# A residual block with Winograd convolutions: columns split by parity, two of six row positions also transformed along columns, PSUM emptied by ScalarE in bf16

## The chip, the cores and the metric

The kernel runs on one core of a Trainium2 chip. The metric is the time of one execution of the whole program on the device, in microseconds; lower is better. Of the kernel before the change there are three timed runs and one execution recorded by the hardware profiler. The engines are named as in the profile: PE is the matrix engine TensorE, PEld its weight loads, DVE is VectorE, ACT is ScalarE, POOL is GpSimd, SP is the engine that issues most transfers.

## What is computed

One residual block of a diffusion network: group norm, SiLU and a 3x3 convolution, an embedding added per channel, group norm, SiLU and a second 3x3 convolution, and the input added at the end. x is [2, 512, 64, 64] in bf16, with 4 groups of 128 channels.

```
def conv3(z, w):
    zp = jnp.pad(z, ((0, 0), (0, 0), (1, 1), (1, 1)))
    taps = [jnp.einsum("bchw,oc->bohw", zp[:, :, i:i+H, j:j+W], w[:, :, i, j]) for i in range(3) for j in range(3)]
    ...
h = conv3(_silu(gn(x, g1, be1)), w1)
h = h + (_silu(t_emb) @ w_emb).reshape(B, C, 1, 1)
h = conv3(_silu(gn(h, g2, be2)), w2)
return x + h
```

## The kernel before

Both convolutions are Winograd transforms F(4,3) along rows: of each six rows of input six combined rows ("positions" 0 to 5) are made, multiplied by six combined weight rows, and the six products are combined into four output rows. Along columns nothing is transformed: the three column taps `kx` are three matmuls with shifted inputs. The channels are cut into four input tiles (`ct`) and four output tiles (`ot`) of 128, each image into two chunks of 32 rows, which are eight row groups. The loops run over the two layers (0 and 1 in the code; "first" and "second" in words), in each over four chunks (two images of two chunks), and over four output tiles. One output tile of one chunk is 6 positions x 4 `ct` x 3 `kx` = 72 matmuls of 128 x 128 by 512 columns (`mm`, L628), accumulated in six PSUM accumulators of one bank each (`ps_acc`, 6 buffers, one per position). There are 32 such tiles.

Beside the matmuls run these parts:

- `prep_U` (L288 to L352) makes the combined weights of one (`ot`, `ct`): a load, nine transposes on PE (L299, L302), two ACT copies out of PSUM (L303, L305), six DVE operations (L328 to L336). The U tiles of a whole layer stay resident.
- `produce_V` (L386 to L473) makes the six positions of one chunk's input: a load of 33 rows (of x, or of the intermediate `h_scr` in HBM), one silu on ACT with the group norm's scale and bias (L415) into one of two buffers `a_tmp`, and 14 DVE operations per `ct` (L454 to L472; in the first chunk L434 to L451, where ACT does the scalings). V tiles are double-buffered.
- `evac` (L632 to L702) empties the accumulators and makes four output rows: ACT copies positions 1 and 3 out as f32 (L635, L649), DVE does the rest in f32 with ten operations (14 in the second layer, where x is added: L674, L675, L678, L681). In the first layer DVE also sums (`accum_out`) and one ACT pass squares (L697); the result goes to `h_scr`. In the second it goes to the output (L702).
- Statistics of the first image (`stats0`) are products on PE (L199 gram, L206 column sums), for the first `ct` a sum on ACT (L212), with a short chain DVE, POOL, DVE that ends in `sc_all` and `nb_all` (L163 to L181). Those of the second image (`gn1_stats_bg`) are 16 ACT passes of 2048 elements (L212, L216).

The order of the work: `_Background` holds generators with a deadline and runs a step of them between two accumulators (`tick`), at a rate that the deadlines set. Then a list scheduler orders each engine's instructions, so that some of them stand ahead of their place in the program. The queue of each engine is worked off in that order. For the first output tile of all, the matmuls go `ct` by `ct` through all six accumulators, so that PE can begin with the first input tile; in all others, position by position.

## Time and profile before

| what | value |
|---|---|
| time, median of three runs | 566.75 us (566.36 to 567.83) |
| span of the profiled execution | 564.7 us |
| first and last matmul of L628 | starts 26.3 us, ends about 558.7 us |
| end of the first output tile | 47.5 us |
| chunks of the first layer begin at | 26.3, 101.1, 169.0, 232.0 us |
| the second layer begins at | 297.4 us |

The span is what the profiler saw of one execution; the timed runs include some 2 us around it. In a row of the profile's groups, "out<-in 128x512" is a tile's name and its shape, "x16" a count, and after the bar stand the busy time and the mean duration. Rows of one engine may overlap: where instructions follow each other without a gap, the distance of their starts is less than the duration that is shown for one.

### The profile page before, as it was taken

What the parts mean: (1) busy time and instruction counts of PE and PEld (TensorE: products, weight loads), DVE (VectorE), ACT (ScalarE), POOL (GpSimd) and SP (SyncE); (2) the same over time, 40 slices, a digit from 0 to 9 for tenths busy, and PEclk for the clock granted to TensorE, in tenths of its full rate; (3) what the DMA queues carried; (4) which work ended last, traced back from release to release, by engine and by line L of the source; (5) the groups of instructions that cost most, each with busy time, mean ns of one, the idle gap of its engine ahead of it and who ended that gap; (6) DMA issues with size and microseconds to landing.
All of it is one profiled execution on the core that took longest, in us unless ns stands there. A gap on an engine that the chain in (4) does not pass through costs nothing.

```text
span 564.7 us, 7699 instructions
## 1 busy us (share of the span) xinstructions
PE 540.7 (96%) x2814; PEld 259.3 (46%) x2814; DVE 479.8 (85%) x1226; ACT 218.3 (39%) x252; POOL 23.3 (4%) x74
## 2 busy tenths in 40 slices
PE   4879999899999999999999989999999999999995
PEld 4535544344444444444445545444444444444442
DVE  2889999989988884898879999999999998555665
ACT  5699999463435332343235314322230300000000
POOL 1110000011001100000000011000000000000000
PEclk9999999999999999999999999999999999999999
DMA  8506654333523120132133512323433122222210
GB/s 336 207 22 216 192 176 139 137 114 124 161 76 108 56 105 37 45 127 96 42 101 102 160 37 76 112 80 123 153 102 101 47 75 74 75 74 76 74 39 37
DMA packets 18754, 59.83 MB, mean 106 GB/s; under 512 B 2075, under 2 KB 3227, under 8 KB 18331
## 3 DMA queue, kind: packets, MB, share of 16 engines
q1 hardware_dynamic: 18656, 59.32, 31.5%
q8 instruction: 22, 0.36, 0.3%
q14 instruction: 17, 0.14, 0.1%
q10 hardware_dynamic: 59, 0.01, 0.0%
HBM read 42.54 MB, written 16.78 MB: 105 GB/s over the span
## 4 chain that ended last, share of the span: by engine, by line
PE 72%; DVE 21%; issue 2%; DMA 2%; ACT 1%; POOL 1%; SPq 0%; DVEq 0%; ACTq 0%
PE acc L628 70%; DVE U L336 2%; DVE U L334 2%; DVE U L329 1%; DMA xbuf<-in_x_dram 1%; DVE U L330 1%; POOL rstd L178 1%; DVE cc L333 1%; PE pa L299 1%; ACT V_146 L212 1%; DMA wn<-in_w_dram 1%; DVE vq L455 1%; DVE yst L662 1%; DVE tt L666 1%; DVE ss L667 0%
## 5 line engine op out<-in xcount | busy, mean ns | idle before, releaser
L628 PE MATMUL acc<-V,U 128*128 128x512 bf16 x2016 | 444.9, 381 | 2.6 <-DVE V L457 1.6
L628 PEld LDWEIGHTS <-U 128*128 128x128 bf16 x2304 | 224.0, 98 | 273.4 <-issue 7.0
L628 PE MATMUL acc<-V_146,U 128*128 128x512 bf16 x288 | 66.4, 381 | 3.2 <-DVE V_146 L448 3.1
L697 ACT ACTIVATE junk<-yst 128x2048 bf16<-128x2048 bf16 x16 | 30.5, 1909 | 58.5 <-DVE yst L693 53.2
L303 ACT COPY U<-pa 128x768 bf16<-128x768 bf16 x32 | 25.7, 803 | 41.1 <-PE pa L299 41.1
L415 ACT ACTIVATE a_tmp_105<-src,nb_all,sc_all 128x2112 bf16<-128x2112 bf16 x14 | 30.1, 2152 | 22.2 <-DVE V L470 18.9
L415 ACT ACTIVATE a_tmp_106<-src,nb_all,sc_all 128x2112 bf16<-128x2112 bf16 x14 | 30.1, 2151 | 21.5 <-DVE vq L455 10.4
L299 PEld LDWEIGHTS <-wn 128*128 128x128 bf16 x192 | 16.5, 142 | 8.0 <-issue 2.9
L299 PE MATMUL pa<-ident,wn 128*128 128x128 bf16 x192 | 16.9, 225 | 2.6 <-DVE tot L165 2.3
L334 DVE SCALAR_TENSOR_TENSOR U<-g1t,cc 128x384 bf16<-128x384 bf16 x32 | 17.5, 546 | 0.0
L333 DVE SCALAR_TENSOR_TENSOR cc<-U 128x384 f32<-128x384 bf16 x32 | 17.5, 546 | 0.0
L336 DVE SCALAR_TENSOR_TENSOR U<-g1t,cc 128x384 bf16<-128x384 bf16 x32 | 17.5, 546 | 0.0
L305 ACT COPY g1t<-pb 128x384 bf16<-128x384 bf16 x32 | 15.8, 495 | 0.4 <-DVE U L336 0.4
L216 ACT ACTIVATE xt<-xt 128x2048 bf16<-128x2048 bf16 x8 | 15.4, 1928 | 0.1
L212 ACT ACTIVATE xt<-xt 128x2048 bf16<-128x2048 bf16 x8 | 15.4, 1928 | 0.0
L199 PE MATMUL gr<-xbuf 128*128 128x128 bf16 x96 | 7.5, 243 | 6.5 <-DMA xbuf<-in_x_dram 6.5
L693 DVE SCALAR_TENSOR_TENSOR yst<-acc,ss 128x512 bf16<-128x512 f32 x16 | 10.9, 682 | 2.5 <-PE acc L628 2.5
L457 DVE TENSOR_TENSOR V<-vq 128x528 bf16<-128x528 bf16 x28 | 11.8, 422 | 0.0
L472 DVE TENSOR_TENSOR V<-V,vq 128x528 bf16<-128x528 bf16 x28 | 11.8, 421 | 0.0
L464 DVE TENSOR_TENSOR V<-vs,vq 128x528 bf16<-128x528 bf16 x28 | 11.8, 421 | 0.0
L466 DVE TENSOR_TENSOR V<-vs,vq 128x528 bf16<-128x528 bf16 x28 | 11.8, 421 | 0.0
L469 DVE TENSOR_TENSOR V<-V,vq 128x528 bf16<-128x528 bf16 x28 | 11.8, 421 | 0.0
(660 smaller groups left out, 594.6 us busy)
## 6 DMA issues: line engine op xcount, KB each, us to landing
wn<-in_w_dram SPq DMA_DIRECT2D x32, 288.0 KB, 3.1
src<-h_scr SPq DMA_DIRECT2D x16, 528.0 KB, 3.9
h_scr<-yst SPq DMA_DIRECT2D x16, 512.0 KB, 2.6
xr<-in_x_dram SPq DMA_DIRECT2D x16, 512.0 KB, 4.1
out_dram<-yst SPq DMA_DIRECT2D x16, 512.0 KB, 3.6
src<-in_x_dram SPq DMA_DIRECT2D x12, 528.0 KB, 4.5
xt<-in_x_dram SPq DMA_DIRECT2D x8, 512.0 KB, 3.7
xbuf<-in_x_dram SPq DMA_DIRECT2D x3, 1024.0 KB, 6.2
```

The costliest lines, as they stand in the source:

```text
L212: nc.scalar.activation(out=o, in_=pc, func=ACT.Identity, accum_out=part[:, k:k + 1])
L216: nc.scalar.activation(out=pc, in_=pc, func=ACT.Square, scale=float(HW) ** -0.5, accum_out=part[:, k:k + 1])
L299: nc.tensor.transpose(pa[:, kx, j, :], wn_v[:, kx, 2 * j, :], ident[:])
L303: nc.scalar.copy(out=U[:, :, 0:NPOS:NPOS - 1, :], in_=pa[:])
L305: nc.scalar.copy(out=g1t[:], in_=pb[:])
L333: nc.vector.scalar_tensor_tensor(out=cc[:], in0=g0, scalar=0.25, in1=g2, op0=ALU.mult, op1=ALU.add)
L334: nc.vector.scalar_tensor_tensor(out=U[:, :, 3, :], in0=g1t[:], scalar=0.5, in1=cc[:], op0=ALU.mult, op1=ALU.add)
L336: nc.vector.scalar_tensor_tensor(out=U[:, :, 4, :], in0=g1t[:], scalar=-0.5, in1=cc[:], op0=ALU.mult, op1=ALU.add)
L415: nc.scalar.activation(out=at[:, a_ - r0:b_ - r0, 1:W + 1], in_=ap, func=ACT.Silu, bias=nb_all[:, layer, b, ct:ct + 1], scale=sc_all[:, la ...
L457: nc.vector.tensor_tensor(out=Vc[:, 1], in0=p_, in1=q, op=ALU.add)
L628: nc.tensor.matmul(accs[pos][:], lhsT=U[ct][:, kx, pos, :], rhs=V[:, ct, pos, :, kx:kx + W], start=first, stop=last)
L697: nc.scalar.activation(out=junk[:], in_=yf, func=ACT.Square, scale=float(HW) ** -0.5, accum_out=ssq[:, ch:ch + 1])
```

## The change

Columns are split by parity: a row of 64 is kept as 32 even and 32 odd ones. Positions 1 and 2 are then also transformed along columns by F(2,3): four combined planes (`vw`, 32 columns each) replace three shifted products of 64 columns. Their weights (`UW`) get the matching four combinations. Positions 3, 4, 0 and 5 keep their three taps; of the taps, `kx` 0 and 2 read both parities in one matmul of 512 columns, and `kx` 1 is two matmuls of 256, each writing every second run of 32 in the accumulator.

One output tile of one chunk is now four groups. Groups 0 and 1 (`mm_w`, L587) are 16 matmuls of 256 columns each; groups 2 and 3 (`mm_d`, L603 and L609) are 16 of 512 and 16 of 256 each. Each group fills an accumulator of two banks, of which there are three. ACT copies a whole accumulator (1024 columns) to bf16 (L623, L630, L636, L644); the rest of the output transform is bf16 on DVE (L627 to L646). The sums of the first layer are two ACT passes of 2048 (L656, L657); in the second layer four ACT copies of 512 (L662) put the columns back in order, one DVE addition adds x (L665), and one transfer stores (L666).

`produce_V` works on pairs of input tiles (`cp`). In the first layer each `ct` has four silus of 512 and one of 64 for the halo row (L349, the line of a helper), in the second one of 2048 and one of 64; both `ct` of a pair lie in the one buffer `at`. Then 15 DVE operations of 1024 or 2048 elements work on the pair (L397 to L438). The V tiles (`vw`, `v34`, `v05`) have three buffers, of which a chunk uses two. `prep_U` also goes by pairs: 18 transposes, three ACT copies of 768 (L290), 11 DVE operations (L294 to L307). The buffers for weight loads and temporaries are halved in number, x of the first image lies in U buffers, and the statistics of the second image (L230, L231) load into the buffers of `produce_V`. `h_scr` is kept in the new layout, and each load of it is followed by one of the halo row (L388, L391). In the first layer all four column sums of the first image are products on PE, emptied by ACT (L495).

The diff, cut to its core:

```diff
-    upool = ctx.enter_context(tc.tile_pool(name="U", bufs=4 * CT))
-    stage = ctx.enter_context(tc.tile_pool(name="stage", bufs=4))
-    wtmp = ctx.enter_context(tc.tile_pool(name="wtmp", bufs=2))
-    vpool = ctx.enter_context(tc.tile_pool(name="V", bufs=2))
+    upool = ctx.enter_context(tc.tile_pool(name="U", bufs=CT))
+    stage = ctx.enter_context(tc.tile_pool(name="stage", bufs=2))
+    wtmp = ctx.enter_context(tc.tile_pool(name="wtmp", bufs=1))
+    vpool = ctx.enter_context(tc.tile_pool(name="V", bufs=3))
+    apool = ctx.enter_context(tc.tile_pool(name="A", bufs=1))
...
-    ps_acc = ctx.enter_context(tc.tile_pool(name="ps_acc", bufs=6, space=PSUM))
+    ps_acc = ctx.enter_context(tc.tile_pool(name="ps_acc", bufs=3, space=PSUM))
...
-            xt = stg.tile([P, hp], BF16, tag="xr")
+            xt = srcp.tile([P, CR + 2, W], BF16, tag="src")
...
+    def produce_V(layer, b, ch, resident=None):
...
+        for cp in range(CP):
+            at = apool.tile([P, 2, AT], BF16, tag="at")
...
+                        for q in range(2):
+                            silu_rows(
+                                _ap(at, i * AT + f * PL + q * HF, [(2 * PL, 2), (W, TR), (1, HF)]),
+                                _ap(sbase, m_off + 2 * f * W + q, [(W, 2), (TH * W, TR), (2, HF)]),
+                                layer, b, ct)
...
+            tq = otmp.tile([P, 2, 2, NT], BF16, tag="tq")
+            VV.tensor_scalar(out=tq[:], in0=_ap(at, 0, [(2 * PL, 2), (AT, 2), (1, NT)]),
+                             scalar1=4.0, scalar2=None, op0=ALU.mult)
+            VV.tensor_tensor(out=tq[:], in0=tq[:], in1=_ap(at, PL, [(2 * PL, 2), (AT, 2), (1, NT)]), op=ALU.subtract)
+            q_, p_ = (_ap(tq, k * 2 * NT, [(W, 2 * TR), (HF, 2), (1, HF)]) for k in range(2))
+            VV.tensor_tensor(out=rows64(layer, zrow[:, 0], 2 * TR), in0=p_, in1=q_, op=ALU.add)
+            VV.tensor_tensor(out=rows64(layer, zrow[:, 1], 2 * TR), in0=p_, in1=q_, op=ALU.subtract)
...
+            e0, o0, om, e1 = E_OFF[layer], O_OFF[layer], O_BEG[layer], E_OFF[layer] + 1
+            VV.tensor_tensor(out=vwm(1), in0=zr(e0), in1=zr(o0), op=ALU.add)
+            VV.tensor_tensor(out=vwm(2), in0=zr(o0), in1=zr(e0), op=ALU.subtract)
+            VV.tensor_tensor(out=vwm(0), in0=zr(om), in1=zr(o0), op=ALU.subtract)
+            VV.tensor_tensor(out=vwm(3), in0=zr(e1), in1=zr(e0), op=ALU.subtract)
...
+            VV.tensor_tensor(out=elo[:], in0=_ap(at, PL, [(PL, 2), (AT, 2), (1, NT)]),
+                             in1=_ap(at, 0, [(2 * PL + NT, 2), (AT, 2), (1, NT)]), op=ALU.subtract)
+            VV.tensor_tensor(out=ehi[:], in0=_ap(at, W, [(3 * PL - W, 2), (AT, 2), (1, NT)]),
+                             in1=_ap(at, PL, [(PL, 2), (AT, 2), (1, NT)]), op=ALU.subtract)
+            VV.tensor_scalar(out=e12[:], in0=elo[:, 0], scalar1=2.0, scalar2=None, op0=ALU.mult)
+            s2 = _ap(e12, 0, [(W, 2 * TR), (HF, 2), (1, HF)])
+            r_ = _ap(ehi, 2 * NT, [(W, 2 * TR), (HF, 2), (1, HF)])
+            VV.tensor_tensor(out=rows64(layer, v34[:, 0], 2 * TR), in0=r_, in1=s2, op=ALU.add)
+            VV.tensor_tensor(out=rows64(layer, v34[:, 1], 2 * TR), in0=r_, in1=s2, op=ALU.subtract)
+            yield
+            VV.tensor_scalar(out=elo[:], in0=elo[:], scalar1=4.0, scalar2=None, op0=ALU.mult)
+            VV.tensor_tensor(out=rows64(layer, v05, 4 * TR),
...
-    SLOTS = NPOS
-    MARGIN = 3
+    SLOTS = 4
+    MARGIN = 2
...
-                def mm(pos, ct, kx, first, last):
-                    nc.tensor.matmul(
-                        accs[pos][:], lhsT=U[ct][:, kx, pos, :], rhs=V[:, ct, pos, :, kx:kx + W],
-                        start=first, stop=last)
+                def mm_w(acc, pair, ct, first, last):
+                    vw = V[ct // 2][0]
+                    c = ct % 2
+                    for k, m in enumerate(pair):
+                        for s in range(2):
+                            lo = UM[m] * 2 * P + s * P
+                            nc.tensor.matmul(
+                                acc[:, k, s * HT:(s + 1) * HT], lhsT=U[:, ct, lo:lo + P],
+                                rhs=vw[:, m, s, c * TR:(c + 1) * TR, :],
+                                start=first and s == 0, stop=last and s == 1)
+
+                def mm_d(acc, which, ct, first, last):
+                    vd = V[ct // 2][1 + which]
+                    c = ct % 2
+                    for k in range(2):
+                        base = vd[:, k if which == 0 else 1 - k]
+                        row = c * TR * RP
+
+                        def u(kx):
+                            lo = UW_N + (kx * 4 + 2 * which + k) * P
+                            return U[:, ct, lo:lo + P]
+                        for kx in (0, 2):
+                            nc.tensor.matmul(
+                                acc[:, k, :], lhsT=u(kx),
+                                rhs=_ap(base, row + (1 if kx == 2 else 0), [(RP, TR), (HF + 1, 2), (1, HF)]),
+                                start=first and kx == 0, stop=False)
+                        offs = (O_OFF[layer], E_OFF[layer]) if layer == 0 else (E_OFF[layer], O_OFF[layer])
+                        for par in range(2):
+                            nc.tensor.matmul(
+                                _ap(acc[:, k], par * HF, [(W, TR), (1, HF)]), lhsT=u(1),
+                                rhs=_ap(base, row + offs[par], [(RP, TR), (1, HF)]),
+                                start=False, stop=last and par == 1)
...
+                    if g == 0:
+                        i_a = nc.scalar.activation(out=mw[:, 1:3, :], in_=acc[:], func=ACT.Copy, scale=0.5 * KAPPA)
+                        if not first_evac:
+                            first_evac.append(i_a)
+                        lo_op, hi_op = ((ALU.subtract, ALU.add) if layer == 0 else (ALU.add, ALU.subtract))
+                        VV.tensor_tensor(out=mw[:, 0, :], in0=mw[:, 1, :], in1=mw[:, 2, :], op=lo_op)
+                        VV.tensor_tensor(out=mw[:, 1, :], in0=mw[:, 1, :], in1=mw[:, 2, :], op=hi_op)
+                    elif g == 1:
+                        nc.scalar.activation(out=mw03[:], in_=acc[:], func=ACT.Copy, scale=KAPPA)
+                        VV.tensor_tensor(
+                            out=_ap(y14, 0, [(HF, 2), (W, 2 * TR), (1, HF)]),
+                            in0=_ap(mw, 0, [(NT, 2), (HF, 2 * TR), (1, HF)]),
+                            in1=_ap(mw03, 0, [(NT, 2), (HF, 2 * TR), (1, HF)]), op=ALU.add)
+                    elif g == 2:
+                        nc.scalar.activation(out=y14[:, 2:4, :], in_=acc[:], func=ACT.Copy, scale=KAPPA)
+                        VV.tensor_tensor(out=qt[:, 0:2, :], in0=y14[:, 0::2, :], in1=y14[:, 1::2, :], op=ALU.add)
+                        VV.tensor_tensor(out=qt[:, 2:4, :], in0=y14[:, 0::2, :], in1=y14[:, 1::2, :], op=ALU.subtract)
+                        VV.tensor_scalar(out=yst[:, 1, :], in0=qt[:, 1, :], scalar1=4.0, scalar2=None, op0=ALU.mult)
+                        VV.tensor_scalar(out=yst[:, 2, :], in0=qt[:, 3, :], scalar1=2.0, scalar2=None, op0=ALU.mult)
+                        VV.tensor_tensor(out=yst[:, 1:3, :], in0=yst[:, 1:3, :], in1=qt[:, 0::2, :], op=ALU.add)
+                        VV.tensor_scalar(out=qt[:, 3, :], in0=qt[:, 3, :], scalar1=8.0, scalar2=None, op0=ALU.mult)
+                    else:
+                        nc.scalar.activation(out=y05[:], in_=acc[:], func=ACT.Copy)
+                        VV.tensor_tensor(out=y05[:], in0=y05[:], in1=qt[:, 0::2, :], op=ALU.add)
+                        VV.tensor_tensor(out=yst[:, 0::3, :], in0=y05[:], in1=qt[:, 1::2, :], op=ALU.add)
+                        finish()
...
+                    if layer == 0:
+                        ssum, ssq = st2[(b, ot)]
+                        nc.sync.dma_start(out=h_scr[b, ot][:, ch].rearrange("p f n -> p (f n)"), in_=yf)
+                        nc.scalar.activation(out=tf, in_=yf, func=ACT.Identity, accum_out=ssum[:, ch:ch + 1])
+                        nc.scalar.activation(out=tf, in_=yf, func=ACT.Square, scale=float(HW) ** -0.5,
+                                             accum_out=ssq[:, ch:ch + 1])
+                    else:
+                        for k in range(2):
+                            for q in range(2):
+                                nc.scalar.copy(
+                                    out=_ap(tmp, k * W + q, [(2 * W, 2), (TH * W, TR), (2, HF)]),
+                                    in_=_ap(yst, 2 * k * NT + q * HF, [(NT, 2), (W, TR), (1, HF)]))
+                        VV.tensor_tensor(out=xr[:], in0=xr[:], in1=tf, op=ALU.add)
+                        nc.sync.dma_start(out=out_v[b, ot][:, ch * CR * W:(ch + 1) * CR * W], in_=xr[:])
...
+                    accs = [new_acc() for _ in range(3)]
+                    for ct in range(CT):
+                        for g in range(3):
+                            groups[g](accs[g], ct, ct == 0, ct == CT - 1)
+                    for g in range(3):
+                        evac(g, accs[g])
+                        bg.tick()
+                    done = 3
```

The order of three places. First, DVE in the start. Here L438 makes the last planes of the first input pair (`v_319`), L300 to L307 are weights, L213 to L186 the statistics of the third and fourth input tile, and L397 begins the second pair. After the change:

```order
L438 TENSOR_TENSOR v_319<-ehi,elo 128x32x2x32
L300 TENSOR_SCALAR g1t<-g1t 128x768
L305 TENSOR_TENSOR g0t<-U 128x2x256
L301 TENSOR_TENSOR U<-U,g1t 128x2x3x128
L306 TENSOR_TENSOR U<-g0t,U 128x2x256
L302 TENSOR_TENSOR U<-U,g1t 128x2x3x128
L307 TENSOR_TENSOR U<-g0t,U 128x2x256
L213 SCALAR_TENSOR_TENSOR jk,me_369<-acc,ident 128x128
L170 COPY tot<-ps 128x2
```

In the kernel before, on DVE at the transition from the second input tile (`vq_111`) to the third (`a_tmp_105`):

```order
L450 TENSOR_TENSOR V_146<-V_146,vt 128x528
L451 TENSOR_TENSOR V_146<-V_146,vt 128x528
L165 COPY tot<-ps 128x2
L167 SCALAR_TENSOR_TENSOR negvar<-tot 128x1
L171 TENSOR_SCALAR negvar<-negvar 128x1
L180 TENSOR_TENSOR sc_all<-rstd,gb 128x1
L440 TENSOR_TENSOR vs<-a_tmp_105 128x1056
L181 SCALAR_TENSOR_TENSOR nb_all<-tot,sc_all,gb 128x1
```

Before, the statistics of single input tiles stand between the transforms of single input tiles; after, both of the second pair stand behind the whole first pair and its weights.

Second, ACT where the passes over the second image stand (L212 and L216 before, L230 and L231 after). Before, in chunk 0, among the weights' copies (L303, L305), the evacuations (L635) and a squaring pass (L697):

```order
L216 ACTIVATE xt,part<-xt 128x2048
L303 COPY U<-pa 128x3x2x128
L635 ACTIVATE c_808<-acc 128x512
L212 ACTIVATE xt,part<-xt 128x2048
L305 COPY g1t<-pb 128x384
L303 COPY U<-pa 128x3x2x128
L697 ACTIVATE junk,ssq_536<-yst 128x2048
```

After, from the end of chunk 0's fourth output tile into chunk 1, among the evacuations (L636, L644, L623, L630) and the finish passes (L656, L657):

```order
L636 ACTIVATE y_1196<-acc 128x1024
L230 ACTIVATE xt,part<-xt 128x2048
L644 ACTIVATE y_1197<-acc 128x1024
L231 ACTIVATE xt,part<-xt 128x2048
L230 ACTIVATE xt,part<-xt 128x2048
L623 ACTIVATE mw<-acc 128x1024
L231 ACTIVATE xt,part<-xt 128x2048
L230 ACTIVATE xt,part<-xt 128x2048
L630 ACTIVATE mw_1389<-acc 128x1024
L231 ACTIVATE xt,part<-xt 128x2048
L656 ACTIVATE tmp,ssum_1193<-yst 128x2048
```

All 16 passes have moved behind the weights' copies of chunk 0 and stand one or two between two evacuations.

Third, ACT at the end of chunk 1, where the input of chunk 2 is made (L349 is the silu; the rows of the second pair begin behind `mw_1939`):

```order
L623 ACTIVATE mw<-acc 128x1024
L630 ACTIVATE mw_1939<-acc 128x1024
L349 ACTIVATE at<-src,nb_all,sc_all 128x2x8x32 x4
L349 ACTIVATE at<-src,nb_all,sc_all 128x64
L349 ACTIVATE at<-src,nb_all,sc_all 128x2x8x32 x2
L656 ACTIVATE tmp,ssum_985<-yst 128x2048
L349 ACTIVATE at<-src,nb_all,sc_all 128x2x8x32
L657 ACTIVATE tmp,ssq_986<-yst 128x2048
L349 ACTIVATE at<-src,nb_all,sc_all 128x2x8x32
L349 ACTIVATE at<-src,nb_all,sc_all 128x64
L636 ACTIVATE y_1936<-acc 128x1024
```

Before, the silus stood singly between evacuations:

```order
L697 ACTIVATE junk,ssq_1179<-yst 128x2048
L415 ACTIVATE a_tmp_105<-src,nb_all,sc_all 128x33x64
L415 ACTIVATE a_tmp_106<-src,nb_all,sc_all 128x33x64
L635 ACTIVATE c_1510<-acc 128x512
L697 ACTIVATE junk,ssq_536<-yst 128x2048
```

The silus of a chunk now come in two blocks of two input tiles, with finish passes inside the second.

More of the change, by code (lines that the diff above doesn't have):

```diff
@@ L60, in drain, with _ap @@
             self._run(self.tasks[0])
+def _ap(base, off, dims):
+    ap = base[:] if not isinstance(base, bass.AP) else base
+    return bass.AP(ap.tensor, ap.offset + off, [tuple(ap.ap[0])] + [tuple(d) for d in dims])
 @with_exitstack
@@ L354 @@
+    UM = (0, 1, 3, 2)
     EMB_PIECE = 2
@@ L590 @@
                 if o2 is not None:
[L591 to L596 removed]
+                    for cp in range(CP):
+                        t_U[(1, o2, cp)] = bg.add(prep_U(1, o2, cp), U_STEPS, slot_of(1, 0, o2) - MARGIN)
+                for cp in range(CP):
+                    if (layer, ot, cp) in t_U:
+                        bg.finish(t_U[(layer, ot, cp)])
@@ L728 @@
+                for g in range(done, 4):
+                    acc = new_acc()
+                    for ct in range(CT):
+                        groups[g](acc, ct, ct == 0, ct == CT - 1)
+                    bg.tick()
+                    evac(g, acc)
             if layer == 0 and ch == NCH - 1:
```

599 lines of the change are left out of this document (218 added, 381 removed).

## The prediction

> **What bounds the kernel now.** I first read the page's busy shares and the chain that ended last, then one table by stage.
>
> ```profile
> PE 540.7 (96%) x2814; PEld 259.3 (46%) x2814; DVE 479.8 (85%) x1226; ACT 218.3 (39%) x252; POOL 23.3 (4%) x74
> PE 72%; DVE 21%; issue 2%; DMA 2%; ACT 1%; POOL 1%; SPq 0%; DVEq 0%; ACTq 0%
> 346.75 206.73 PE acc L628 x948
> ```
>
> TensorE carries the chain, and its longest piece is an unbroken run of matmuls: 206.73 / 948 = 0.218 us for one of 512 columns. An output tile of 72 takes 15.70 us, and 32 of them 502.4 us of the span of 564.7. What the shares hide is where TensorE doesn't run; the next table has the matmuls of L628 alone, cut at the ends of the first output tile and of the chunks.
>
> ```profile
> core 0: us, PE busy (x), PEclk, DMA share, GB/s
> 26.30:47.50 21.20, 16.36 (x72) 1.00 0.10 27
> 47.50:101.10 53.60, 49.87 (x217) 1.00 0.62 197
> 101.10:169.00 67.90, 64.06 (x288) 1.00 0.37 119
> 169.00:232.00 63.00, 63.00 (x288) 1.00 0.19 69
> 232.00:297.40 65.40, 63.51 (x290) 1.00 0.28 89
> 297.40:369.00 71.60, 64.63 (x288) 1.00 0.31 99
> ```
>
> A chunk of 288 matmuls needs 62.8 us, and the middle chunks need 63.0 to 67.9. So almost nothing is lost after 47.5 us: a shorter matmul list pays in full, and a wait longer than before costs in full. Before 47.5, and in the first chunk, all three engines are full:
>
> ```profile
> core 0: us, PE busy (x) PEld busy (x) DVE busy (x) ACT busy (x) POOL busy (x), PEclk, DMA share, GB/s
> 47.50:101.10 53.60, 53.43 (x310) 26.86 (x309) 53.60 (x140) 53.45 (x67) 0.63 (x3) 1.00 0.62 197
> ```
>
> **The gain: matmuls.** An output tile goes from 72 matmuls of 512 columns to 32 of 512 and 64 of 256. A 256 does not occur before; the nearest rows are the 128-column products of the statistics and the 512.
>
> ```profile
> 12.42 1.96 PE L199 MATMUL gr<-xbuf 128*128 128x128 bf16 x32
> 14.22 1.46 PE L206 MATMUL cs<-xbuf,ones_bf 128*128 128x512 bf16 x6
> 26.31 1.03 PE L628 MATMUL acc<-V_146,U 128*128 128x512 bf16 x4
> ```
>
> 32 of them, each with a weight load of its own, take 1.96 us, 0.061 each. A line through 0.061 and 0.218 gives 0.1135 for 256; half of 0.218 is 0.109, the cheapest, and 0.218 (no gain from the shorter row) the dearest. I take 0.1135, nearest to the rows on either side. A tile costs 32 x 0.218 + 64 x 0.1135 = 14.24, 1.46 less, and 32 tiles save **46.8 us**. The 252 transposes behind the first tile stay (15.4).
>
> **What the vector work costs.** Prices are distances from one start to the next in unbroken runs, since rows overlap.
>
> ```profile
> 93.51 0.69 DVE L459 TENSOR_TENSOR vs<-a_tmp_106 128x1056 bf16<-128x1056 bf16 x1
> 94.13 0.42 DVE L454 TENSOR_SCALAR vq<-a_tmp_106 128x1056 bf16<-128x1056 bf16 x1
> 94.47 0.41 DVE L467 TENSOR_TENSOR V<-a_tmp_106 128x528 bf16<-128x528 bf16 x1
> ...
> 95.78 0.41 DVE L457 TENSOR_TENSOR V<-vq 128x528 bf16<-128x528 bf16 x1
> 96.12 0.42 DVE L458 TENSOR_TENSOR V<-vq 128x528 bf16<-128x528 bf16 x1
> ...
> 558.51 0.68 DVE L678 TENSOR_TENSOR yst<-c_5279,xr 128x512 bf16<-128x512 f32 x1
> 559.12 0.68 DVE L681 TENSOR_TENSOR yst<-t_5293,xr 128x512 bf16<-128x512 f32 x1
> 559.72 0.68 DVE L689 TENSOR_TENSOR yst<-acc,tt 128x512 bf16<-128x512 f32 x1
> 560.32 0.68 DVE L701 TENSOR_TENSOR yst<-acc,ss 128x512 bf16<-128x512 f32 x1
> 561.02 0.33 SPq L702 DMA_DIRECT2D out_dram<-yst  x1
> ```
>
> A bf16 addition of 1056 costs 0.62, of 528 0.34, so 0.61 for 1024 and 1.14 for 2048; a scaling of 1056 costs 0.34 and of 2048 about 0.61; an f32 operation of 512 costs 0.60. The output transform of a tile was 10 of these f32 operations (6.0; 14 and 8.4 in the second layer) and becomes 4.9 and 6.1. By these prices VectorE loses about 60 us of work in all. ScalarE gets the opposite:
>
> ```profile
> 18.24 2.15 ACT L415 ACTIVATE a_tmp_105<-xbuf,nb_all,sc_all 128x2112 bf16<-128x2112 bf16 x1 [0.41 <-DVE nb_all L181]
> 20.29 0.78 ACT L303 COPY U<-pa 128x768 bf16<-128x768 bf16 x1
> ...
> 21.34 1.09 ACT L434 ACTIVATE vq<-a_tmp_105 128x1056 bf16<-128x1056 bf16 x1
> 22.32 0.59 ACT L235 ACTIVATE junk_333<-cs 128x512 bf16<-128x512 f32 x1
> ...
> 22.89 0.65 ACT L442 ACTIVATE vt<-vs 128x528 bf16<-128x528 bf16 x1
> 23.43 0.65 ACT L443 ACTIVATE vt<-vs 128x528 bf16<-128x528 bf16 x1
> ...
> 78.76 0.78 ACT L303 COPY U<-pa 128x768 bf16<-128x768 bf16 x1
> 79.44 0.48 ACT L305 COPY g1t<-pb 128x384 bf16<-128x384 bf16 x1
> 79.81 0.61 ACT L649 ACTIVATE c_1089<-acc 128x512 f32<-128x512 f32 x1
> 80.30 1.92 ACT L216 ACTIVATE xt<-xt 128x2048 bf16<-128x2048 bf16 x1
> 82.10 0.21 ACT L216 ACTIVATION_READ_ACCUMULATOR xt<-xt 128x1 f32 x1
> 82.19 1.92 ACT L212 ACTIVATE xt<-xt 128x2048 bf16<-128x2048 bf16 x1
> ```
>
> A PSUM copy of 768 costs 0.68, of 384 0.37, so the new one of 1024 costs 0.68 + 256 x 0.00081 = 0.89. A pass of 2048 with a sum costs 1.89. The SBUF rows of 1056 (0.98) and 528 (0.54) differ by 0.00084 per element; from the silu of 2112 (2.05) that leaves 0.70 for a silu of 512 and 0.32 for a halo row of 64. A tile of the first layer then takes 4 x 0.89 + 2 x 1.89 = 7.3 of ScalarE where it took 2 x 0.49 + 1.89 = 2.9, and an input pair 2 x (4 x 0.70 + 0.32) = 6.2. The second layer also gets a small load per input tile for the halo row; SP issues one in 0.33 (the last row above) and has 0% of the chain, so I cost it at nothing; without that cover it is one landing, some 4 us, per chunk. ScalarE is under TensorE's 14.24 per tile, so the mean is hidden; what counts is where its queue is dense.
>
> **The start: +20.5.** Three accumulators are opened at once and fed tile by tile of input, so output tile 0 can't end before the second input pair is transformed. By the new VectorE order the statistics of the third and fourth input tile stand behind the whole first pair and the weights. The first pair's silu ends at about 25.8 (before, the second silu came at 27.25; the third and fourth statistics were interleaved). Then VectorE needs 0.61 + 1.14 + 1.14 + 1.22 + 1.14 + 1.22 = 6.5 to the first two W planes: first matmul near 32.3, where it was 26.31. Another 7.7 of planes and weight operations end near 40; statistics and the power on GpSimd to 42 and 43; silu of two tiles, 6.2, to 49.1; VectorE 6.5 to 55.6 and 4.6 more for the last planes; the last group and 36 transposes end near **66.5** against 47.5. That is +19.0, or +20.5 of waiting beside the 1.5 saved.
>
> **The rest of chunk 0: 53.5** (3 x 14.24 + 6.6 of transposes + 4.2 of waits for weights), against 53.6. VectorE, full before, has 26 us of weights, 20 of output transforms and 22 of the next input in this stretch and a few us more than it lasts.
>
> **Chunk 1: 76.5 against 67.9.** Two parts. First, the one `at` buffer makes a chain at the boundary: silu of the second pair, with two finish passes among it (6.2 + 3.8), then 6.5 of VectorE; about 7.5 of it lies beyond the end of the tile. Second, the 16 passes over the second image (16 x 1.89 = 30.2) now stand in ScalarE's queue between evacuations, where nearly all of them stood under chunk 0 before. With 10 evacuations (8.9) and 4 finish passes (7.6) that is 46.7 us, in which TensorE has 10 groups of 3.56, 35.6. Three accumulators allow it two groups of lead, but ScalarE enters late by about as much, so I charge 12, from bounds of 4 (lead kept) and 13. 57.0 + 7.5 + 12 = 76.5.
>
> **Chunk 2: 71.0 against 63.0.** Its silu is behind those passes. From near 182: 11.8 for the first pair with passes and evacuations between, 4.0 until VectorE has read `at`, 10.0 for the second pair, 6.5 to its W planes: about 213 to 214, some 14 after the last matmul of chunk 1 can have ended.
>
> **Chunk 3 to the end.** Chunk 3 and the first chunk of the second layer hold 8 x 14.24 + 8.8 of transposes + 3 = 125.7 (before 65.4 + 71.6 = 137.0). Three more chunks: 170.9 + 3 x 2 of boundary = 176.9; bounds 0 and 5 each. The tail was 6.0 behind the last matmul; now copy 1.0, three VectorE steps 1.3, four ScalarE copies of 512 at 0.54, an addition of 1.14 and the store's 3.7 make 9.4.
>
> Sum: 66.5 + 53.5 + 76.5 + 71.0 + 125.7 + 176.9 + 9.4 = 579.5 of span, 14.8 over the 564.7 of the profiled execution. The three timed runs have a median 2.05 above that span, so the time is about **582 us**.
>
> **Rivals.** *A, faster: the accumulators absorb it.* If TensorE never waits for ScalarE or the input after tile 0, only the start and the tail stay: 66.5 + 31 x 14.24 + 15.4 + 9.0 (the waits that before has outside its start: 564.7 - 47.5 - 31 x 15.70 - 15.4 - 6.0) + 9.4 = 541.7, 544 as a time. It is decided between the fourth tile of chunk 0 and the second of chunk 1: does ScalarE hold 46.7 us of work while TensorE has 35.6? For it: ScalarE's busy share was 39%. Against it: in 47.50:101.10 the same passes filled ScalarE with 53.45 of 53.60 already, and each tile now brings 4.4 more.
>
> *B, VectorE at half rate on odd offsets.* In the second layer the planes start one element off; 10,240 elements of a pair have such an operand. If those run at twice the price, a pair costs 5.3 more; about 10.6 of that falls on the dense stretch around that layer's first chunk and 5.3 on each of two boundaries: 603. None of the rows above starts its operands so, and the trace doesn't say. [...]
>
> *C, strided PSUM writes.* The 1024 half-row matmuls of L609 write every other run of 32. If each took 0.218, the gain shrinks by 1024 x 0.1045 = 107: 689. No row of before writes so. [...] That the change does not do what it says (a 256 at the price of a 512) would show the same way.
>
> **How the numbers follow.** Forecast 0.68, A 0.20, B 0.08, C 0.04. The forecast's own range is 560 to 600: the 12 of chunk 1 between 4 and 13, the 14 of chunk 2 and 20.5 of the start by a quarter, boundaries between 0 and 5. The range reaches into A down to 552 and past B to 608; left out are the lower half of A, C, and some of the ends, 0.2. A difference under 0.3% (565.05 to 568.45) is no change for a measurement here; 0.05 of the forecast lies there. Faster 0.20, same 0.05, slower 0.75.
>
> **What would show it.** The last matmul of tile 0 near 66; L587 and L609 at 0.11 apart; TensorE's waits named after the copies L623 to L644 in chunk 1 and after W planes at the starts of chunks 1 and 2; chunks 1 and 2 of 77 and 71 us, later ones near 59; 9 us behind the last matmul. Wrong if chunk 1 takes 60 (A), if L412 to L415 take longer in the second layer than in the first (B), or if L609 is dearer than L587 (C).

## The result and the profile after

The changed kernel takes 583.25 us (median of four runs, 581.84 to 584.12) where the kernel before takes 566.56 beside it: a ratio of 1.0287, 95% interval 1.0266 to 1.0307. The profiled execution spans 582.3 us, 17.6 more than before. The forecast was 582.

First the page's shares of busy time and the chain, as before:

```profile
PE 519.1 (89%) x3590; PEld 339.5 (58%) x3590; DVE 450.4 (77%) x937; ACT 383.5 (66%) x459; POOL 29.2 (5%) x90
DVE 30%; PE 20%; ACT 10%; issue 4%; POOL 1%; ACTq 0%; DVEq 0%
```

TensorE's share of the span falls from 96% to 89%, and the chain that ended last is no longer mostly its own (72% before, 20% now). ScalarE's busy time goes from 218.3 to 383.5 us. The table by stage shows where that counts; it is cut at the first matmul of the convolutions, the end of output tile 0, the starts of the chunks, and the end of the last matmul (the three last chunks in one row).

```profile
core 0: us, PE busy (x) PEld busy (x) DVE busy (x) ACT busy (x) POOL busy (x), PEclk, DMA share, GB/s
35.70:70.70 35.00, 23.25 (x136) 14.77 (x136) 28.78 (x64) 20.72 (x31) 1.69 (x5) 0.71 0.23 68
70.70:118.70 48.00, 47.75 (x364) 32.50 (x362) 46.76 (x101) 34.91 (x41) 1.10 (x4) 1.00 0.30 96
118.70:199.10 80.40, 68.10 (x431) 42.38 (x430) 49.63 (x119) 73.38 (x87) 5.50 (x14) 0.87 0.41 122
199.10:262.30 63.20, 60.07 (x395) 38.77 (x393) 55.14 (x120) 49.33 (x59) 7.02 (x16) 0.97 0.26 80
262.30:329.50 67.20, 62.54 (x441) 41.19 (x439) 58.59 (x120) 49.02 (x52) 1.68 (x6) 0.97 0.31 107
329.50:398.50 69.00, 64.93 (x484) 43.51 (x483) 66.34 (x160) 42.76 (x52) 5.75 (x14) 1.00 0.30 101
398.50:572.30 173.80, 172.84 (x1153) 111.29 (x1151) 127.72 (x216) 95.41 (x113) 2.74 (x11) 1.00 0.27 93
572.30:582.30 10.00, 0.00 (x0) 0.00 (x0) 2.61 (x3) 3.59 (x5) 0.00 (x0) 0.62 0.13 53
```

Beside the forecast:

| stage | forecast | measured |
|---|---|---|
| start to end of tile 0 | 66.5 | 70.7 |
| rest of chunk 0 | 53.5 | 48.0 |
| chunk 1 | 76.5 | 80.4 |
| chunk 2 | 71.0 | 63.2 |
| chunk 3 and first chunk of the second layer | 125.7 | 136.2 |
| three last chunks | 176.9 | 173.8 |
| behind the last matmul | 9.4 | 10.0 |
| sum | 579.5 | 582.3 |

The sum is near by errors that cancel: six of the seven terms are off by 3 to 10.5 us, three up and three down. Where TensorE runs undisturbed, the matmuls are at the price of the forecast. From its timeline at the end of chunk 0 (start, duration, count):

```profile
104.41 3.66 PE L587 MATMUL acc<-vw,U 128*128 128x256 bf16 x32
107.90 0.61 PE L603 MATMUL acc<-v,U 128*128 128x512 bf16 x2
108.34 0.39 PE L609 MATMUL acc<-v,U 128*128 128x256 bf16 x2
108.57 0.61 PE L603 MATMUL acc<-v,U 128*128 128x512 bf16 x2
```

32 of L587 take 107.90 - 104.41 = 3.49 us, 0.109 each. Two of 512 with two of L609 take 0.67, so a strided one of 256 costs (0.67 - 0.436) / 2 = 0.117. A tile is 3.49 + 16 x 0.67 = 14.2; in the second layer such a four takes 0.68 and a tile 14.38. So the 46 us of matmuls are gained, and some 63 are lost elsewhere.

The view of what TensorE waited for:

```profile
PE ps L168 <- DVE jk L213: 7.7, 2, 6.5
PE pt L289 <- ACT g0t L290: 6.6, 3, 3.5
PE acc L587 <- DVE vw L412: 4.8, 1, 4.8
PE ps L168 <- DVE me L237: 4.1, 2, 3.2
PE acc L603 <- ACT y L644: 2.8, 2, 1.8
PE acc L603 <- ACT mw L623: 2.4, 2, 2.2
```

Behind the first load no wait is longer than 6.5 us, and those named after evacuations (L623 to L644) are small. The 6.5 is a statistic in tile 0 that stands in VectorE's queue. Two others are ScalarE's, though they bear other names: the products of L168 that wait 4.1 for the second image's statistics (L237), and a transpose that waits 3.5 for a weight copy (L290, in chunk 3), stand in TensorE's queue ahead of matmuls, and what they need stands in ScalarE's queue. That queue in chunk 1:

```profile
121.27 1.00 ACT L636 ACTIVATE y<-acc 128x1024 bf16<-128x1024 f32 x1
122.17 1.90 ACT L230 ACTIVATE xt<-xt 128x2048 bf16<-128x2048 bf16 x1
...
124.07 1.00 ACT L644 ACTIVATE y<-acc 128x1024 bf16<-128x1024 f32 x1
124.97 1.90 ACT L231 ACTIVATE xt<-xt 128x2048 bf16<-128x2048 bf16 x1
...
158.48 1.00 ACT L623 ACTIVATE mw<-acc 128x1024 bf16<-128x1024 f32 x1
159.38 1.90 ACT L230 ACTIVATE xt<-xt 128x2048 bf16<-128x2048 bf16 x1
...
165.06 1.90 ACT L231 ACTIVATE xt<-xt 128x2048 bf16<-128x2048 bf16 x1
...
166.95 1.01 ACT L630 ACTIVATE mw<-acc 128x1024 bf16<-128x1024 f32 x1
```

From the first pass to the last, 122.17 to 166.95, it stands still only once for more than 0.1 us, for 1.18.

### The profile page after: what moved, and what is told of

The parts are those of the page before. It is cut to its first block, busy times and chain, and to the rows that moved or that the text cites. A ratio compares the mean times of both kernels' runs of the same rounds, so it can differ in the third digit from the quotient of the medians.

```text
span 582.3 us, 9166 instructions
## 1 busy us (share of the span) xinstructions
PE 519.1 (89%) x3590; PEld 339.5 (58%) x3590; DVE 450.4 (77%) x937; ACT 383.5 (66%) x459; POOL 29.2 (5%) x90
## 4 chain that ended last, share of the span: by engine, by line
DVE 30%; PE 20%; ACT 10%; issue 4%; POOL 1%; ACTq 0%; DVEq 0%
PE acc L603 10%; PE acc L609 5%; PE acc L587 4%; ACT at L349 3%; ACT tmp L662 3%; DVE tq L399 2%; DVE y L645 2%; DVE yst L641 2%; DVE elo L427 2%; DVE ehi L429 1%; DVE v L438 1%; DVE qt L638 1%; DVE yst L646 1%; DVE qt L637 1%; DVE xr L665 1%
## 5 line engine op out<-in xcount | busy, mean ns | idle before, releaser
L603 PE MATMUL acc<-v,U 128*128 128x512 bf16 x1024 | 318.0, 392 | 5.2 <-ACT y L644 2.8
L609 PE MATMUL acc<-v,U 128*128 128x256 bf16 x1024 | 205.7, 281 | 0.0
L609 PEld LDWEIGHTS <-U 128*128 128x128 bf16 x1024 | 100.7, 99 | 129.5 <-issue 8.1
L587 PE MATMUL acc<-vw,U 128*128 128x256 bf16 x1024 | 128.4, 281 | 9.5 <-DVE vw L412 4.8
L587 PEld LDWEIGHTS <-U 128*128 128x128 bf16 x1024 | 102.7, 101 | 26.0 <-issue 10.9
L603 PEld LDWEIGHTS <-U 128*128 128x128 bf16 x1024 | 99.8, 98 | 27.0 <-issue 3.4
L349 ACT ACTIVATE at<-src,nb_all,sc_all 128x512 bf16<-128x512 bf16 (+2 forms) x92 | 79.1, 914 | 19.7 <-DVE ehi L429 12.9
L644 ACT ACTIVATE y<-acc 128x1024 bf16<-128x1024 f32 x32 | 32.5, 1016 | 65.5 <-PE acc L609 65.5
L662 ACT COPY tmp<-yst 128x512 bf16<-128x512 bf16 x64 | 42.1, 757 | 18.9 <-DVE yst L646 18.9
L636 ACT ACTIVATE y<-acc 128x1024 bf16<-128x1024 f32 x32 | 32.5, 1015 | 23.4 <-PE acc L609 23.4
L623 ACT ACTIVATE mw<-acc 128x1024 bf16<-128x1024 f32 x32 | 32.6, 1019 | 12.4 <-PE acc L587 6.6
L656 ACT ACTIVATE tmp<-yst 128x2048 bf16<-128x2048 bf16 x16 | 30.5, 1907 | 10.2 <-DVE yst L646 8.2
L289 PE MATMUL pt<-ident,wn 128*128 128x128 bf16 x288 | 25.1, 234 | 13.0 <-ACT g0t L290 6.6
L630 ACT ACTIVATE mw<-acc 128x1024 bf16<-128x1024 f32 x32 | 32.6, 1019 | 5.8 <-PE acc L587 5.8
L637 DVE TENSOR_TENSOR qt<-y 128x1024 bf16<-128x1024 bf16 x32 | 21.9, 685 | 17.6 <-ACT y L636 17.5
L657 ACT ACTIVATE tmp<-yst 128x2048 bf16<-128x2048 bf16 x16 | 30.5, 1905 | 0.2
L665 DVE TENSOR_TENSOR xr<-xr,tmp 128x2048 bf16<-128x2048 bf16 x16 | 19.6, 1223 | 12.3 <-ACT tmp L662 12.1
```

Source lines behind the costliest of these rows:

```text
L289: nc.tensor.transpose(pt[:, i, kx, :], wns[i][:, ky, kx, :], ident[:])
L349: nc.scalar.activation(out=at_ap, in_=in_ap, func=ACT.Silu, bias=nb_all[:, layer, b, ct:ct + 1], scale=sc_all[:, layer, b, ct:ct + 1])
L587: nc.tensor.matmul(acc[:, k, s * HT:(s + 1) * HT], lhsT=U[:, ct, lo:lo + P], rhs=vw[:, m, s, c * TR:(c + 1) * TR, :], start=first and s == ...
L603: nc.tensor.matmul(acc[:, k, :], lhsT=u(kx), rhs=_ap(base, row + (1 if kx == 2 else 0), [(RP, TR), (HF + 1, 2), (1, HF)]), start=first and ...
L609: nc.tensor.matmul(_ap(acc[:, k], par * HF, [(W, TR), (1, HF)]), lhsT=u(1), rhs=_ap(base, row + offs[par], [(RP, TR), (1, HF)]), start=Fal ...
L623: i_a = nc.scalar.activation(out=mw[:, 1:3, :], in_=acc[:], func=ACT.Copy, scale=0.5 * KAPPA)
```

## The experiments

Times are medians; each ratio is to runs of the kernel before on the same chip. "Chunk 0" in this part is the rest of it behind tile 0.

**No passes over the second image.**

```diff
-            nc.scalar.activation(out=pieces[k], in_=pieces[k], func=ACT.Identity, accum_out=part[:, k:k + 1])
-            nc.scalar.activation(out=pieces[k], in_=pieces[k], func=ACT.Square, ...)
+            nc.vector.tensor_reduce(out=part[:, 2 * k:2 * k + 2], in_=pieces[k][:, 0:4]..., op=ALU.max, axis=AX.X)
```

> The 16 ScalarE passes over the second image are left out (its group norm gets numbers from four elements instead), all else stays. In the changed kernel chunk 1 lasts from 118.6 to 199.1 us (80.5), with ScalarE back to back from 121.3 to 171.3. Theory Q (ScalarE's queue holds the accumulators): chunk 1 falls to 60 to 64 us, TensorE's waits there nearly vanish, and the granted clock of that chunk goes from 0.87 to 0.97 or more; the time falls by 15 to 20 us, to 563 to 568. Rival I (the input of chunk 1 and 2, with its single buffer, is what TensorE waits for): chunk 1 stays above 74 and the time falls by less than 6 us.

566.13 us, ratio 0.9981 (0.9964 to 0.9999). Chunk 1 and 2 of its table by stage:

```profile
117.70:184.30 66.60, 61.73 (x431) 38.93 (x430) 51.62 (x132) 46.73 (x59) 5.29 (x14) 0.97 0.45 151
184.30:247.30 63.00, 60.14 (x395) 38.43 (x393) 56.71 (x122) 48.87 (x57) 6.25 (x16) 0.97 0.25 85
```

Chunk 1 falls by 13.8 to 66.6, not quite to the expected 64; chunk 3 falls by 3.6. The passes cost 17 us of time, as much as the kernel became slower, so theory Q holds in what it said of the time. How they cost it is only in part what it said: TensorE's waits in chunk 1 fall from 12.2 to 4.9 us, and busy time lost to a lower granted clock (summed over windows of half a microsecond) from 8.6 to 1.7, about as much. The 4.9 us of waits that are left are mostly for the input (2.6) and for statistics (1.7).

**Statistics ahead of the first transform.**

```diff
-    for cp in range(CP):
-        stats0(2 * cp)
...
+    stats0(0)
+    next(gen_V0)
+    stats0(1)
+    next(gen_V0)
+    stats0(2)
+    stats0(3)
...
```

> The statistics of the third and fourth input tile are written ahead of the transform of the first pair, so that on VectorE they stand among its planes and not behind them and the weights. Theory S (their place in VectorE's queue sets the end of output tile 0): silu of the second pair begins at 37 to 39 instead of 46.8 us, held then by the one buffer, and tile 0 ends 7 to 9 us earlier than 70.8; the time falls by 6 to 9 us, to 574 to 577. Rival L (the late landing of x at 9.95 us is what counts): tile 0 ends less than 2 us earlier.

577.07 us, 1.018 (1.0142 to 1.0218). Tile 0 ends at 64.1, 6.6 earlier, and everything behind it moves along. The place of the third tile's statistic (L213) on VectorE in the changed kernel, right behind the last weight operation (L307), and the second pair's silu there:

```profile
43.48 0.42 DVE L307 TENSOR_TENSOR U<-g0t,U 128x512 bf16<-128x512 bf16 x1
43.82 0.28 DVE L213 SCALAR_TENSOR_TENSOR jk<-acc,ident 128x128 f32<-128x128 f32 x1
46.83 6.41 ACT L349 ACTIVATE at<-U,nb_all,sc_all 128x512 bf16<-128x512 bf16 x10 [1.95 <-POOL rstd L183]
```

That silu in this run:

```profile
39.34 6.42 ACT L349 ACTIVATE at<-U,nb_all,sc_all 128x512 bf16<-128x512 bf16 x10
```

It begins at 39.3 where it began at 46.8, behind the first pair's reads of the one buffer. Theory S holds; tile 0 gained a little less than the 7 to 9 us that it promised.

**First input tile loaded first.**

```diff
-    next(gens_U0[0])
     ...
             xres.append(xt)
+            if ct == 0:
+                next(gens_U0[0])
```

> The load of the first input tile is issued ahead of the first two weight loads. In the changed kernel it landed at 9.95 us, in the kernel before at 6.49. If its place behind two weight loads is the cause: it lands at 6 to 7, the first silu begins some 3 us earlier, and tile 0 ends 2 to 3.5 us earlier (time 580 to 581). If the statistics' place in VectorE's queue takes it up again, the time moves by less than 1 us.

578.37 us, 1.0203 (1.0163 to 1.0243). TensorE's first row in this kernel and in the changed one:

```profile
5.78 2.53 PE L203 MATMUL acc<-U 128*128 128x128 bf16 x22 [5.78 <-DMA U<-in_x_dram]
```

```profile
9.95 0.93 PE L203 MATMUL acc<-U 128*128 128x128 bf16 x7 [9.95 <-DMA U<-in_x_dram]
```

The load lands 4.2 us earlier, and tile 0 ends 5.6 earlier (65.1), more than the 2 to 3.5 that were expected: the first pair's silu, in two halves in the changed kernel (20.71 to 23.88 and 27.35 to 30.52), here runs in one piece from 18.43 and ends 5.8 earlier. Two weight loads stood ahead of x, since weights are now loaded by pairs; in the kernel before it was one, and x landed at 6.49. What the second load costs by itself was not tried, as this run moves both.

**No finish passes in chunk 3.** The two ScalarE passes of L656 and L657 are replaced by constants where `idx` is the last chunk's.

> The two ScalarE passes that sum and square a finished tile are left out in chunk 3 alone (its sums are set to constants). Chunk 3 and the first chunk of the second layer took 136.1 us, 10.4 more than forecast, with TensorE's longest wait there, 3.55 us, for a weight copy on ScalarE that stood behind such passes. Theory C (the weight copies wait in ScalarE's queue and hold TensorE's transposes, and the matmuls behind them): the two chunks take 129 or less, the time falls by 6 us or more. Rival D (VectorE is full there, busy 124.8 of 136.1): they fall by less than 3 us.

579.38 us, 1.0221 (1.0183 to 1.0259). Chunk 3 falls from 67.2 to 63.1, and the second layer's first chunk stays (69.6). So 132.7 for both, between the theories: the finish passes ahead of weight copies cost chunk 3 some 4 us, and the chunk behind it nothing. TensorE's longest wait in chunk 3 falls from 3.55 to 1.08 us, and the granted clock there rises from 0.97 to 1.00.

**Few weight operations in the second layer.** The eleven VectorE operations become a fill of the W weights and three scalings.

> In the second layer's weight preparation most VectorE work is left out: the eleven operations of a pair (4.4 us) become one fill and three scalings (about 1.4), with the transposes and ScalarE copies as they were. Without the finish passes of chunk 3 only chunk 3 became shorter (67.2 to 63.1 us); the second layer's first chunk stayed at 69 (69.0 to 69.6), with VectorE busy 66.3 of it. Theory D (VectorE is the bound of that chunk): it falls from 69.0 to 62 to 65, time down by 4 to 8 us. Rival C (weight copies in ScalarE's queue, or transposes behind them): it stays above 67.

581.0 us, 1.0247 (1.0206 to 1.0287). The second layer's first chunk took 68.0, 1.0 less, with VectorE busy 58.9 of it and not 66.3. Rival C's number, then; but no wait for a weight copy of more than 0.83 us is left there. What remains are 90 transposes (some 5 us), a wait of 1.9 for a statistic, and small ones. VectorE's weight work there is not what costs.

**Sums on VectorE.**

```diff
-  VV.tensor_tensor(out=yst[:, 1:3, :], in0=yst[:, 1:3, :], in1=qt[:, 0::2, :], op=ALU.add)
+  VV.scalar_tensor_tensor(out=yst[:, 1:3, :], in0=yst[:, 1:3, :], scalar=1.0, in1=qt[:, 0::2, :],
+                          op0=ALU.mult, op1=ALU.add, accum_out=...)
   ...
-  nc.scalar.activation(out=tf, in_=yf, func=ACT.Identity, accum_out=ssum[:, ch:ch + 1])
```

> The summing pass of ScalarE per first-layer tile (1.89 us) is taken away; two of VectorE's additions that make the tile sum as they go instead (about 0.5 us more each). Theory Q (ScalarE's queue is what is too long in chunks 1 and 3): chunk 1 falls by about 2 x 1.9 to 4 x 1.9 us, chunk 3 by some 2, and the time by 5 to 10 us. Rival D (VectorE is as full, so 1.0 us more per tile costs as much): the time stays within 2 us.

578.07 us, 1.0194 (1.0174 to 1.0215). Chunk 1 falls by 6.0 to 74.4, chunk 3 not at all (67.3). In chunk 1 ScalarE is what is short (busy 68.3 of these 74.4 us). In chunk 3 VectorE seems to take back what ScalarE saves: each of the two summing additions lasts 1.21 us in place of 0.69, a silu waits 4.4 us for VectorE's last read of the one buffer, and the weight copy behind that silu now holds TensorE for 4.85 us.

**Passes spread.** The passes load into the buffer `xr`, one half at a time, and their due times are earlier.

```diff
-            xt = srcp.tile([P, CR + 2, W], BF16, tag="src")
+            xt = ypool.tile([P, CR * W], BF16, tag="xr", bufs=1)
...
-                               slot_of(0, 1, 0) + SLOTS * ct)
+                               slot_of(0, 0, 1) + 1 + 3 * ct)
```

> The 16 passes over the second image stay on ScalarE but get a buffer of their own (the one that holds x in the second layer, unused in the first), and due times four to sixteen steps earlier, so that most stand in chunk 0, where ScalarE was busy 34.8 of 47.8 us. Theory Q (their place, not their number, is the cost): chunk 1 falls from 80.4 to 64 to 70, chunk 0 grows by less than 4, the time falls by 9 to 15 us, to 568 to 574. Rival (the total of ScalarE's work counts, wherever it stands): chunk 0 grows by what chunk 1 loses, and the time falls by less than 4.

571.55 us, 1.0084 (1.0061 to 1.0108). Chunks 0 and 1:

```profile
69.20:135.80 66.60, 53.27 (x370) 34.33 (x368) 57.59 (x133) 65.36 (x79) 3.85 (x11) 0.95 0.41 136
135.80:195.00 59.20, 58.66 (x426) 38.44 (x424) 52.88 (x116) 51.82 (x65) 2.30 (x8) 1.00 0.40 124
```

The time is in theory Q's range, but not as it said: chunk 0 grew by 18.6 and chunk 1 fell by 21.2. ScalarE is now full in chunk 0 (65.4 of 66.6). Most of the gain is in chunks 2 and 3 (59.0 and 62.2, 9.2 less together). Whether the buffer or the due times make it is not separated.

**All four edits**: statistics first, first load first, sums on VectorE, passes spread.

> A version with the first load moved ahead, the statistics of all four tiles ahead of the first transform, the sums on VectorE and the passes spread. If the four gains add (about 5 + 6 + 11 + 4 us), the time is 553 to 560, below the kernel before the change (566.6). If they lean on the same wait, 562 to 568.

565.75 us, 0.9961 (0.9941 to 0.998). That is in the 562 to 568 expected if the four lean on the same wait, so the gains do not add: chunk 0 took 64.5, with ScalarE busy 57.8 and VectorE 59.6 of it.

**Kept busy.** 28 and 34 products that nobody reads, in front of the second pair's statistics and behind the first pair's matmuls.

> In the changed kernel TensorE ran at half its clock in busy time worth 12.4 us in output tile 0 (6.2 lost) behind waits of 6.45, 2.47 and 2.78 us. Here 62 products that nobody reads are put into two of these waits (28 ahead of the statistics of the second pair, 34 behind the first pair's matmuls). Theory H (the clock falls because TensorE stood still, and the work behind each wait pays): the granted clock between first matmul and end of tile 0 rises from 0.71 to above 0.85, tile 0 ends 2 to 4 us earlier, as half-speed work stands behind the second wait alone on the path; time 579 to 581. Rival (the half clock lies inside time that VectorE sets anyway): clock up, time within 1 us of 583.

583.58 us, 1.03 (1.0273 to 1.0327). The granted clock between 35.0 us and the end of tile 0 rose to 0.96, tile 0 ended 1.2 us earlier, and chunk 1 began at 119.2, 0.5 later than without. Theory H's 579 to 581 us did not come, and the rival holds: in tile 0 the lower clock cost nothing that VectorE had not already set.

**Spread over chunks 0 and 1, with the earlier start.** The edits of the second, third and seventh run, with due times `slot_of(0, 0, 2) + 3 * ct`.

> First load ahead, statistics ahead, and the passes with their own buffer, due four steps later than in the run before, so that they are shared between chunks 0 and 1; the sums stay on ScalarE. In the run with the passes spread, chunk 0 grew by 18.6 us with ScalarE busy 65.4 of 66.6, and chunk 1 fell by 21.2: ScalarE's total in the two chunks counts. Theory T (total of ScalarE over chunks 0 and 1): the two together last 121 to 126 us whatever the place; with the earlier start and later chunks of 59 and 62, the time is 558 to 563. If place counts, they fall to 115 to 119 and the time to 551 to 556.

559.97 us, 0.9892 (0.9861 to 0.9922): 1.1% under the kernel before, by an interval that does not reach 1. Its stages up to chunk 1:

```profile
27.90:59.40 31.50, 22.47 (x145) 14.75 (x144) 30.33 (x59) 23.80 (x33) 2.39 (x5) 0.79 0.29 91
59.40:117.00 57.60, 49.75 (x368) 32.79 (x366) 54.83 (x124) 54.13 (x66) 3.17 (x10) 0.99 0.42 142
117.00:179.50 62.50, 60.60 (x426) 39.09 (x426) 47.77 (x102) 57.80 (x70) 2.70 (x9) 0.98 0.34 115
```

Chunks 0 and 1 last 120.1 together, where 125.8 were needed with the denser placing and 128.4 in the changed kernel. That is between the two cases: neither ScalarE's total alone (121 to 126) nor its place alone (115 to 119) gives it.

**With sums on VectorE for the first image.**

> As the run before, and with the sums on VectorE for the first image only, that is in chunks 0 and 1, where ScalarE is full; chunks 2 and 3 keep them on ScalarE. Theory T: ScalarE has 15 us less in chunks 0 and 1, which last 116 to 121 us, and the time is 553 to 558. If VectorE is as full there (it was busy 59.6 of 64.5 in chunk 0 of the version with all edits), nothing is gained over the run before.

562.99 us, 0.9931 (0.9908 to 0.9954). Chunks 0 and 1 took 121.8. ScalarE had 9 us less in them than in the run before (102.8 against 111.9), and it gained nothing, as the rival said: VectorE was busy 113.1 us in place of 102.6. But TensorE's longest wait there, 6.1 us, is for one evacuation (L637 there), which stands in ScalarE's queue behind a finish pass, four silus and a pass over the second image (111.7 to 117.9). So the place of single instructions counts too; how much of the loss it makes was not tried.

## Why the prediction was right, and where it was not

- **The gain.** 14.24 for a tile is what a tile takes (14.2 and 14.38), in part by luck. The 0.061 on the forecast's line is a row's duration; from start to start that row gives (14.22 - 12.42) / 32 = 0.056, and the line then 0.110 for 256, near the 0.109 of the plain ones. That surplus makes up for the strided ones, which it did not have. Rival C is out: a strided half row costs 0.117 against 0.109 for a plain one, 8 us in all and not 107; whether the stride or the change between shapes makes these 8 was not tried.
- **The start, 70.7 for 66.5.** The mechanism, statistics behind the first pair and its weights, is shown by the second run. The step that failed is the end of the first pair's silu, 30.5 for 25.8: the forecast has no term for a later landing of x, and two weight loads now go ahead of it in the load queue. With x loaded first (third run) that silu ends at 24.7.
- **The rest of chunk 0, 48.0 for 53.5.** The 36 transposes counted with tile 0 were counted here again (36 x 0.061 = 2.2), and the 4.2 of waits for weights are not there: TensorE was busy 47.75 of the 48.0. VectorE's list in the forecast, 26 + 20 + 22 = 68 us, is 14 more than the stretch and not a few; it was busy 46.8 in it. One of the six weight pairs was already made in tile 0 (60.4 to 68.6), and the last input pair was still being made when chunk 1 began. VectorE's relief over the whole kernel was 29 us of busy time (479.8 to 450.4), and not about 60.
- **Chunk 1, 80.4 for 76.5.** ScalarE's passes are the main cause, as forecast, and the first run shows it by taking them away. Their stretch was given as 46.7 us of work and has 47.2, with 1.2 idle (121.3 to 169.7). That the loss came out only 3.9 too small is luck, for its parts are others. The forecast had 7.5 for the input and 12 for the accumulators. Measured are 2.6 for the input, 3.9 for evacuations, 4.1 for the second image's statistics, 1.5 ahead of an embedding product, and 8.6 of busy time lost to a lower granted clock, which the forecast put at nothing. Of its signs, "waits named after the copies L623 to L644" is met by 3.9 of 12.2 us.
- **Chunk 2, 63.2 for 71.0.** Here the step is wrong on its own numbers: the passes were put at an end "near 182", while a start at 121 and 46.7 us make 168. The silus of chunk 2 began at 169.7, in time, and of the 14 us of waiting 3.1 came, none of it for the input.
- **Chunk 3 and the second layer's first, 136.2 for 125.7.** The 3 us of waits were a guess without a row. Above matmuls and transposes, chunk 3 lost some 7 us, of which 4 are from finish passes ahead of weight copies (fourth run), a stretch of half clock among them. The chunk behind it lost some 6, of which 3.9 are five waits of at most 1.9; neither VectorE's weight work (1.0, fifth run) nor the finish passes (nothing, fourth run) are their cause. This stays open.
- **The tail**, 10.0 for 9.4, and the last three chunks, 173.8 for 176.9: that is 2.9 above 12 tiles of 14.24, or 1.2 above 12 of the measured 14.38, for three boundaries at which the forecast had 6.

Rival A was decided where the forecast said, by ScalarE's 46.7 us against TensorE's 35.6. Even without the passes the span was 563.8 and not A's 541.7. Start and tail are in A's sum; what it lacks are waits that have other causes: chunks 1 and 2 still lasted 66.6 and 63.0 us, where their matmuls need 57.0, and the second layer's first chunk 69.0. Rival B is out too: L412 takes 0.69 on average in the first layer and 0.72 in the second, as in the row below, and not double. In the first layer L414 and L415, which also have an operand at an odd offset there, take 0.71 to 0.72. So the signs that the forecast named for B and C are there by their letter, at some 5% and 7%, and the rivals' prices, twice and 0.218, are shown by no run.

```profile
412.80 0.71 DVE L412 TENSOR_TENSOR vw<-zrow 128x1024 bf16<-128x1024 bf16 x1
```

## What to carry to other kernels

When an engine's work is nearly doubled so that another's may shrink, count its queue stretch by stretch and not as a share of the span: ScalarE was busy 66% of the time, and 16 passes in one stretch of 48 us, in which it stood still for 1.2, cost 17 us. Background work that was placed to suit the old balance has to be placed anew: with the same 16 passes spread over two chunks and in a buffer of their own, the kernel was 0.8% slower than before and not 2.9%, and with the two start edits as well it was 1.1% faster. A sum that comes out right does not show that its terms are; compare them one by one. And end a chain of forecasts by adding its own starts and durations once more: one stage's wrong end time was the largest single surplus here.

## What was not expected of the hardware

In windows of half a microsecond, the kernel before shows a granted clock of 1.00 wherever TensorE works. In the changed one it falls to 0.50 behind waits. TensorE's timeline in chunk 1:

```profile
140.56 1.91 PE L587 MATMUL acc<-vw,U 128*128 128x256 bf16 x16
145.71 0.59 PE L168 MATMUL ps<-me,ones_neg 128*128 128x2 f32 x2 [3.23 <-DVE me L237]
146.37 3.57 PE L587 MATMUL acc<-vw,U 128*128 128x256 bf16 x16
149.73 1.06 PE L603 MATMUL acc<-v,U 128*128 128x512 bf16 x2
```

The same 16 matmuls take 1.91 us ahead of a wait of 3.23 and 3.57 behind it; full speed is back at 151.5. In windows of half a microsecond, busy time at half clock loses 6.2 us in tile 0, 8.6 in chunk 1 and 1.7 each in chunks 2 and 3, 18.2 in all. That this is nearly the slowdown is chance as far as tile 0 goes, where taking it away gained nothing; in chunk 1, where ScalarE is full, it was not tried.

Where the half clock begins and ends can be read from the same trace. Cut into tenths of a microsecond, its seven stretches of half clock up to the last matmul begin at 35.42, 55.90, 124.17, 144.65, 158.30, 202.67 and 301.66 us: whole steps of 3.41 us lie between them, and they last one, two or four steps. The next table shows four such steps around the wait of 3.23:

```profile
core 0: us, PE busy (x), PEclk, DMA share, GB/s
141.24:144.65 3.41, 1.24 (x12) 1.00 0.29 83
144.65:148.06 3.41, 2.28 (x11) 0.50 0.42 123
148.06:151.48 3.42, 3.42 (x15) 0.50 0.08 31
151.48:154.89 3.41, 3.41 (x22) 1.00 0.63 196
```

The step ahead of a fall was not always idle: here TensorE was busy 1.24 us of it, and 0 to 1.6 us ahead of all seven falls, while in this trace no step with 1.93 us or more was followed by one (in the kept-busy run one with some 1.9 was). Nor did a fall follow every step with as little work: the first three of the trace, up to 11.53 us, with 0, 0 and 1.58 us, are followed by none. Full clock came back behind steps that were busy for 3.36 us or more, and the half stayed behind steps of 2.45 or less. One long wait was not needed: the fall at 202.67 has only waits of 0.9 and 1.0 us ahead of it.
